# Routed attention and a gated feed-forward block: when and how the weights are converted, and how the first batch is laid out

## The chip, the cores and the metric

The kernel runs on one core of one Trainium2 chip. The core has TensorE for matrix products (PE; PEld is its weight load), VectorE (DVE), ScalarE (ACT) and GpSimd (POOL) for elementwise work, and SyncE (SP), whose queue issues transfers. Each engine takes its instructions in the order of its own queue; engines wait for one another through semaphores. The metric is the device time of one execution in microseconds (us); lower is better.

## The reference

Four batches of eight heads, 768 positions of 64 numbers. Each query and key is assigned to the nearest of 16 centroids of its head (cosine similarity), and a query attends only to keys of its own cluster. The result goes through a feed-forward block (ffn) of width 2048. The weights w_in (512 x 2048) and w_out (2048 x 512) arrive as 64-bit floating point, the rest as 32-bit.

```python
q_assign = np.argmax(np.einsum('bhsd,hcd->bhsc', q_n, c_n), axis=-1)
k_assign = np.argmax(np.einsum('bhsd,hcd->bhsc', k_n, c_n), axis=-1)
mask = q_assign[:, :, :, None] == k_assign[:, :, None, :]
scores = np.where(mask, scale * np.matmul(q, k.transpose(0, 1, 3, 2)), -1e9)
attn = softmax(scores)                  # with 1e-9 in the denominator
x = np.matmul(attn, v)                  # (B,H,S,D) -> (B*S, H*D)
h = x @ w_in
g = h * erf(softplus(h))
out = (g @ w_out).astype(np.float32)
```

## The kernel before

**Pairs, units, chunks.** Two heads are handled together as a pair; 16 pairs (four to a batch), each of 12 units: a half of the queries (384 columns, HW) by one block j of 128 keys, six blocks to a half. The feed-forward block works in 12 chunks of 256 rows, three to a batch.

**Per pair.** `route` (L239) transposes q and k on VectorE (L244), copies a bf16 version of both into the mask operands `qm` and `km` on GpSimd (L246), clears one row of `qm` (L250), multiplies by the centroids (psim, L255), and finds the nearest one with operations on VectorE and one product with `rank` on GpSimd (L262 to L286); the one-hot result goes into `qm` on VectorE (L292) and into `km` on ScalarE (L294). `shift` (L299) makes twelve bf16 products (sm, L306), takes the maximum of each row on VectorE (L310), turns the twelve columns into a row (nm L315, pn L320, nmT L322), and writes this row into `qm` by way of a DRAM tile (two issues, L324 and L327). Together they are `aside(p)`, a generator whose every `yield` is one step: four of `route`, twelve maxima and a last step.

**Per unit.** `scores` (L340): two f32 products and two bf16 mask products into one PSUM tile, Exp on ScalarE (L358) into one of eight `pr` tiles, and a running sum `acc` on GpSimd (L362, L366). The tiles of sc and sm share two PSUM buffers (pool `ps_s`). `attend` (L370) runs once per half: the products with v (av, L377), the row sums (psum, L384), a division made from Ln, Exp and VectorE operations (L390 to L395), and the result xT (L406).

**Feed-forward.** `hidden(n)` (L434) makes h in eight groups (hp, L442, copied out by VectorE, L449) and ends in `gate(n)`: Softplus and Erf on ScalarE (L425), the product on VectorE (L427). `project(n)` (L456) multiplies by w_out (po, L461), copies (L468) and writes out (L469). `ffn_stream` yields the cost of each matmul; chunk n starts only when all four pairs of its batch are done, and the products of `project(n - 1)` are woven into `hidden(n)`.

**Weights.** `convert` (L157) handles 1024 columns of f32 result: a 1 MB load issued from GpSimd's queue (L159) into one of two buffers, Square on ScalarE (L165), and seven VectorE operations (L166 to L185) that put the bits of the 64-bit number together to a 32-bit one. There are 16 such steps, eight for w_in and eight for w_out.

**Order.** `aside(0)` comes first. Then a loop over the units in twos: `attend` of the half before, at j = 2; `scores` twice; in the first four pairs one `convert`, except at j = 2; then five slots (SLOTS), each of which pumps ffn matmuls worth `per_slot` cycles and takes one step of the next pair's `aside`. This is the order in which the program is traced. A scheduler then orders the instructions of each engine by its own estimate of when they are ready, unless an instruction is marked to keep the order of the program; only the load of an activation table (L234) is so marked. The pools of the ffn (`g`, `a_s`, `osb`) are opened at the end of the first batch, where the conversion's buffers are closed (L528, L529), in the same memory.

Of the kernel before, what the change touches and what calls it, by code (L numbers as in the profile page):

```python
# [17 lines left out]
P = 128  # L18
# [14 lines left out]
LC = 1024  # L33
TINY_HI = 2.0**-15 * 1.125
# [6 lines left out]
SLOTS = 5  # L41


@with_exitstack
def kernel(
# [11 lines left out]

    def pool(name, bufs, **kw):
        return ctx.enter_context(tc.tile_pool(name=name, bufs=bufs, **kw))
# [8 lines left out]
    xTp = pool("xTp", 1)  # L68
    linep = pool("linep", 2, space=bass.MemoryType.DRAM)
# [51 lines left out]
    wpool = ExitStack()  # L121
    setup = wpool.enter_context(tc.tile_pool(name="setup", bufs=1))
    cen = setup.tile([P, D], F32, name="cen")
# [4 lines left out]
    nc.vector.tensor_copy(out=identb, in_=ident)  # L128
    nc.vector.memset(minus, -1.0)

    for c in range(C):
        nc.vector.memset(rank[0:D, c : c + 1], float(C - c))
        nc.vector.memset(rank[D:P, c : c + 1], BIG * (C - c))
    nc.vector.memset(ccT, 0.0)
    nc.vector.memset(alleps, S * EPS)

    for e in range(2):
        nc.vector.reduce_sum(
            out=own[:, e : e + 1],
            in_=ident.rearrange("p (g x c) -> p x g c", x=2, c=C)[:, e], axis=AX.XY,  # L140
        )
    for t in lows:
        nc.gpsimd.memset(t["q"], 0.0)
        nc.gpsimd.memset(t["k"], 0.0)
        for e in range(2):
            nc.gpsimd.memset(t["k"][e * D + SH : e * D + SH + 1, e], 1.0)
    for t in prs:
        nc.gpsimd.memset(t[:, :, HW : HW + 2], EPS)
# [5 lines left out]
    wraw = wpool.enter_context(tc.tile_pool(name="wraw", bufs=2))  # L154
    wtmp = wpool.enter_context(tc.tile_pool(name="wtmp", bufs=2))

    def convert(dst, src):  # L157
        raw = wraw.tile([P, LC, 2], U32, name="raw64")
        nc.gpsimd.dma_start(out=raw.rearrange("p (a n) w -> p a (n w)", a=src.shape[1]), in_=src)  # L159
        hi, lo = raw[:, :, 1], raw[:, :, 0]  # L160
        m = wtmp.tile([P, LC], U32, name="w_m")
        x = wtmp.tile([P, LC], U32, name="w_x")
        mf, xf = m.bitcast(F32), x.bitcast(F32)

        nc.scalar.activation(out=xf, in_=raw.bitcast(F32)[:, :, 1], func=ACT.Square)  # L165
        nc.vector.tensor_scalar(  # L166
            out=x.bitcast(I32), in0=xf, scalar1=TINY_HI**2, scalar2=-1.0,
            op0=ALU.is_ge, op1=ALU.mult,
        )

        nc.vector.tensor_scalar(
            out=m, in0=hi, scalar1=3, scalar2=0x7FFFFFFF,
            op0=ALU.logical_shift_left, op1=ALU.bitwise_and,
        )
        nc.vector.scalar_tensor_tensor(  # L175
            out=m, in0=m, scalar=0x40000000, in1=x, op0=ALU.bitwise_xor, op1=ALU.bitwise_and
        )
        nc.vector.tensor_scalar(
            out=x, in0=m, scalar1=0x7F800000, scalar2=None, op0=ALU.bitwise_and
        )  # L180
        nc.vector.scalar_tensor_tensor(
            out=xf, in0=lo, scalar=2.0**-52, in1=xf, op0=ALU.mult, op1=ALU.mult
        )
        nc.vector.tensor_tensor(out=xf, in0=mf, in1=xf, op=ALU.add)
        nc.vector.scalar_tensor_tensor(  # L185
            out=dst.bitcast(U32), in0=hi, scalar=0x80000000, in1=x,
            op0=ALU.bitwise_and, op1=ALU.bitwise_or,
        )

    w_steps = []  # L190
    for c in range(0, DFF, LC):
        for r in range(DM // P):
            rows = moe_w_in[r * P : (r + 1) * P, 2 * c : 2 * (c + LC)]
            w_steps.append((w_in[:, r, c : c + LC], rows.unsqueeze(1)))
    n = LC // DM
# [372 lines left out]
```

The softmax here doesn't subtract the row's maximum and nothing guards it: scores larger than these inputs give would overflow.

## Time and profile before

| | |
|---|---|
| time, median of 6 runs | 1354.16 us (1352.52 to 1356.17) |
| the profiled execution | 1356.17 us, of which 1354.4 us are the span from the first to the last instruction |
| mean granted TensorE clock | 0.943 |
| PE busy | 1190.4 us (88%) |
| DVE busy | 656.9 us (49%) |
| ACT busy | 476.5 us (35%) |
| POOL busy | 414.4 us (31%) |
| chain that ended last | PE 67%, DVE 16%, ACT 8% |
| conversion of weights on DVE | 152 us (sum of the groups of L166 to L185) |
| ffn products on PE (hp, po) | 758 us |

The profile is one execution. Busy times are summed over the span and so over stages with different limits; a matmul's record overlaps its neighbour's, so a busy PE is not PE at its peak. The granted clock is the share of its full speed at which TensorE ran.

### The profile page before, as it was taken

What the parts mean: (1) busy time and instruction counts of PE and PEld (TensorE: products, weight loads), DVE (VectorE), ACT (ScalarE), POOL (GpSimd) and SP (SyncE); (2) the same over time, 40 slices, a digit from 0 to 9 for tenths busy, and PEclk for the clock granted to TensorE, in tenths of its full rate; (3) what the DMA queues carried; (4) which work ended last, traced back from release to release, by engine and by line L of the source; (5) the groups of instructions that cost most, each with busy time, mean ns of one, the idle gap of its engine ahead of it and who ended that gap; (6) DMA issues with size and microseconds to landing.
All of it is one profiled execution on the core that took longest, in us unless ns stands there. A gap on an engine that the chain in (4) does not pass through costs nothing.

```text
span 1354.4 us, 12507 instructions
## 1 busy us (share of the span) xinstructions
PE 1190.4 (88%) x4881; PEld 629.6 (46%) x4881; DVE 656.9 (49%) x924; ACT 476.5 (35%) x516; POOL 414.4 (31%) x310
## 2 busy tenths in 40 slices
PE   1676676679999899879999989889999999999998
PEld 0122222236546445344554635544644646575764
DVE  5989999974443525441634443442625302221221
ACT  2223222234335425432543633423534524330321
POOL 5335546351424233423233231424242221100000
PEclk9878777879899999989999989989999999999999
DMA  5312243220101011201011010101000000000000
GB/s 121 97 58 71 71 119 86 74 36 1 24 20 32 12 27 25 36 0 32 20 18 26 18 26 16 35 1 32 21 0 28 1 8 8 8 8 8 8 16 15
DMA packets 132875, 42.88 MB, mean 32 GB/s; under 512 B 126640, under 2 KB 126672, under 8 KB 131792
## 3 DMA queue, kind: packets, MB, share of 16 engines
q1 hardware_dynamic: 129488, 25.31, 9.2%
q0 software_dynamic: 3328, 16.78, 3.6%
q8 instruction: 38, 0.62, 0.2%
q14 instruction: 21, 0.17, 0.0%
HBM read 35.73 MB, written 6.34 MB: 31 GB/s over the span
## 4 chain that ended last, share of the span: by engine, by line
PE 67%; DVE 16%; ACT 8%; issue 4%; POOL 3%; DMA 1%; POOLq 0%; DVEq 0%; ACTq 0%
PE po L461 24%; PE hp L442 21%; PE sc L347 8%; PE av L377 7%; PE sm L306 4%; DVE nmx L310 2%; PE sc L353 1%; ACT pr L358 1%; DVE g L427 1%; ACT L390 1%; PE psum L384 1%; ACT km L294 1%; DVE hot L281 1%; POOL acc L366 1%; DVE w_m L175 1%
## 5 line engine op out<-in xcount | busy, mean ns | idle before, releaser
L442 PE MATMUL hp<-xT,w_in 128*128 128x256 f32 x1536 | 383.9, 387 | 2.8 <-DVE g L449 2.8
L461 PE MATMUL po<-w_out,g 128*128 128x512 f32 x768 | 374.3, 607 | 10.4 <-DVE g L449 7.7
L366 POOL TENSOR_TENSOR acc<-acc,pr 128x768 f32<-128x768 f32 x128 | 229.7, 1794 | 451.2 <-ACT pr L358 446.2
L442 PEld LDWEIGHTS hp<-xT,w_in 128*128 128x128 f32 x1536 | 290.3, 193 | 118.7 <-issue 80.7
L358 ACT ACTIVATE pr<-sc 128x768 f32<-128x768 f32 x192 | 151.6, 808 | 323.9 <-PE sc L353 323.2
L310 DVE TENSOR_REDUCE nmx<-sm 128x2 f32<-128x768 f32 x192 | 180.2, 953 | 108.4 <-PE sm L306 107.0
L347 PE MATMUL sc<-qT,kT 64*128 64x384 f32 x768 | 192.6, 558 | 25.2 <-DVE nmx L310 19.0
L461 PEld LDWEIGHTS po<-w_out,g 128*128 128x128 f32 x768 | 142.1, 192 | 130.7 <-issue 104.9
L449 DVE COPY g<-hp 128x512 f32<-128x512 f32 x96 | 65.9, 686 | 237.8 <-PE hp L442 237.8
L377 PE MATMUL av<-pr,in_v 128*64 128x386 f32 x768 | 159.5, 523 | 22.4 <-DVE xT L406 11.4
L306 PE MATMUL sm<-km,qm 128*128 128x384 bf16 x384 | 104.8, 359 | 84.6 <-ACT pr L358 33.7
L347 PEld LDWEIGHTS sc<-qT,kT 64*128 64x128 f32 x768 | 70.5, 201 | 106.9 <-DVE nmx L310 44.1
L306 PEld LDWEIGHTS <-qm 128*128 128x128 bf16 x384 | 36.7, 102 | 166.4 <-issue 152.6
L362 POOL TENSOR_TENSOR acc<-pr,pr 128x768 f32<-128x768 f32 x32 | 61.6, 1926 | 162.3 <-ACT pr L358 161.9
L377 PEld LDWEIGHTS av<-pr,in_v 128*64 128x64 f32 x768 | 56.0, 143 | 109.5 <-issue 94.0
L425 ACT ACT_TABLE_LOAD x48 | 61.6, 1283 | 103.0 <-DVE g L449 102.2
L392 DVE SCALAR_TENSOR_TENSOR den<-psum,inv 128x384 f32<-128x384 f32 x32 | 17.8, 557 | 150.7 <-ACT inv L391 150.7
L427 DVE TENSOR_TENSOR g<-a_s,g 128x512 f32<-128x512 f32 x96 | 67.6, 757 | 23.4 <-ACT a_s L425 23.4
L425 ACT ACTIVATE a_s<-g 128x2048 f32<-128x2048 f32 x24 | 45.9, 1910 | 69.9 <-DVE g L449 69.8
L353 PE MATMUL sc<-qm,km 64*128 64x384 bf16 x384 | 69.9, 342 | 0.0
L294 ACT COPY km<-hotT 32x384 bf16<-32x384 bf16 x64 | 32.5, 508 | 90.3 <-DVE hotT L286 89.6
L425 ACT ACTIVATE a_s<-a_s 128x2048 f32<-128x2048 f32 x24 | 45.8, 1910 | 0.3
(74 smaller groups left out, 723.4 us busy)
## 6 DMA issues: line engine op xcount, KB each, us to landing
raw<-in_moe_w_in_dram POOLq DMA_DIRECT2D x8, 1024.0 KB, 5.7
raw<-in_moe_w_out_dram POOLq DMA_DIRECT2D x8, 1024.0 KB, 5.3
in_q<-in_q_dram SPq DMA_DIRECT2D x64, 96.0 KB
in_k<-in_k_dram SPq DMA_DIRECT2D x64, 96.0 KB
in_v<-in_v_dram SPq DMA_DIRECT2D x32, 192.0 KB
out_dram<-osb SPq DMA_DIRECT2D x24, 256.0 KB
qm<-line SPq DMA_DIRECT2D x32, 1.5 KB
line<-nmT SPq DMA_DIRECT2D x16, 3.0 KB
```

The lines of the kernel that those rows point to most:

```text
L306: nc.tensor.matmul(sm[:, e, 0:HW], lhsT=st["qm"][:, e, t * P : (t + 1) * P], rhs=st["km"][:, e, half * HW : (half + 1) * HW], start=True, ...
L310: nc.vector.tensor_reduce(out=nmx[:, t, half], in_=sm[:, :, 0:HW], axis=AX.X, op=ALU.max, negate=True)
L347: nc.tensor.matmul(sc[:, e, 0:HW], lhsT=st["kT"][r, j * P : (j + 1) * P], rhs=st["qT"][r, cols], start=True, stop=False,)
L353: nc.tensor.matmul(sc[:, e, 0:HW], lhsT=st["km"][r, e, j * P : (j + 1) * P], rhs=st["qm"][r, e, cols], start=False, stop=True,)
L358: nc.scalar.activation(out=pr[:, :, 0:HW], in_=sc[:, :, 0:HW], func=ACT.Exp, scale=D**-0.5)
L366: nc.gpsimd.tensor_tensor(out=st["acc", half], in0=st["acc", half], in1=pr[:, :, 0:HW], op=ALU.add)
L377: nc.tensor.matmul(av[e * D : (e + 1) * D], lhsT=st["v"][:, j, e], rhs=prs[(u0 + j) % NPT][:, e], start=(j == 0), stop=(j == NJ - 1),)
L425: nc.scalar.activation(out=s[:, i : i + half], in_=src[:, i : i + half], func=func)
L427: nc.vector.tensor_tensor(out=h[:, i : i + GW], in0=s[:, i : i + GW], in1=h[:, i : i + GW], op=ALU.mult)
L442: nc.tensor.matmul(hp[:, a], lhsT=w_in[:, r, f0 : f0 + P], rhs=xTs[b * HP + r][c], start=(r == 0), stop=(r == HP - 1),)
L449: nc.vector.tensor_copy(out=gs[n][:, fp * GW : (fp + 1) * GW], in_=hp)
L461: nc.tensor.matmul(po, lhsT=gs[n][:, ft, tt * P : (tt + 1) * P], rhs=w_out[:, ft], start=(ft == 0), stop=(ft == NFT - 1),)
```

## The change

- **Conversion.** A step is 512 columns (LC), 16 steps for w_in and 16 for w_out. In place of Square and seven VectorE operations, a step has Abs on ScalarE, a maximum and an integer addition on GpSimd (`clamp`), and five VectorE operations. The 64-bit data is loaded from SP's queue (`fetch`), for w_in into quarters of the two `g` tiles, for w_out into the half tiles `a_s` of the gates; the results m and x lie in the same places. `convert` is a generator that yields after each VectorE operation; `prepare(n)` takes n of these steps.
- **When.** The 16 steps of w_in are spread over the first aside and the first four pairs, 36 operations before the first scores and then 11 a pair. Those of w_out follow in the second batch, two operations after each pump. `hidden` and `project` are traced no further than the weights are converted.
- **First batch.** The loop over units goes one slot at a time, 12 slots of preparation and 48 with scores; `aside` of the next pair, `prepare` and `attend` (two units behind the scores) have fixed places. `te`, `ve`, `ae` and `ge` mark every instruction they issue to keep the program's order, up to slot 44 (FIRST). Two PSUM tiles alternate for av, one of them from the ffn's pool. In the last four slots the ffn is pumped, 16 matmuls of chunk 0 each.
- **Routing.** The copies into `qm` and `km` and the clearing of the row move from GpSimd to ScalarE. The transposes of q and k are one step. v is loaded before the maxima instead of after. In the later batches the steps of `aside` have chosen slots (ASIDE) out of 30.
- **Mask products.** `scores` takes one or two units; for two it makes the f32 products of both first, then the mask products of both.
- **Feed-forward.** A chunk starts when the halves that it reads are done. `project(0)` is not woven into `hidden(1)` but follows it. The gate has two half tiles instead of one whole; there is one output tile instead of two. `attend` is one unit, and `divide` is split off it, in two steps.

```diff
-LC = 1024
-TINY_HI = 2.0**-15 * 1.125
+LC = 512
+TINY_HI = 2.0**-15
+ASIDE = (0, 2, 4, 6, *range(9, 9 + 2 * NJ), 10 + 2 * NJ)
+FIRST = 2 * NJ * HP - 4
+class InOrder:
+    def __getattr__(self, name):
+        def call(*args, **kw):
+            ins = getattr(self.engine, name)(*args, **kw)
+            if self.on[0]:
+                self.tc.keep_in_program_order(ins)
+            return ins
+        return call
...
-    def convert(dst, src):
-        raw = wraw.tile([P, LC, 2], U32, name="raw64")
-        nc.gpsimd.dma_start(out=raw.rearrange("p (a n) w -> p a (n w)", a=src.shape[1]), in_=src)
...
+    room = [gp.tile([P, NFT, TB], F32, name="g") for _ in range(2)]
+    def fetch(n):
+        if n in steps or n >= len(w_steps):
+            return
+        if n < n_w_in:
+            t = room[n // 2 % 2][:, n % 2 * (NFT // 2) : (n % 2 + 1) * (NFT // 2)]
+        else:
+            t = half_tile()
+        t = t.rearrange("p f t -> p (f t)").bitcast(U32)
+        nc.sync.dma_start(out=t[:, 0 : 2 * LC], in_=w_steps[n][1])
+        raw = t[:, 0 : 2 * LC].rearrange("p (n w) -> p n w", w=2)
+        steps[n] = raw[:, :, 1], raw[:, :, 0], t[:, 2 * LC : 3 * LC], t[:, 3 * LC : 4 * LC]
+    def clamp(n):
+        if n < len(w_steps):
+            hi, _, _, x = steps[n]
+            ae.activation(out=x.bitcast(F32), in_=hi.bitcast(F32), func=ACT.Abs)
+            ge.tensor_scalar(
+                out=x.bitcast(F32), in0=x.bitcast(F32), scalar1=TINY_HI, scalar2=None, op0=ALU.max
+            )
+            ge.tensor_tensor(
+                out=x.bitcast(I32), in0=x.bitcast(I32), in1=bias.to_broadcast([P, LC]), op=ALU.add
+            )
+    def convert():
+        clamp(0)
+        clamp(1)
+        for n in range(len(w_steps)):
+            hi, lo, m, x = steps[n]
+            mf, xf = m.bitcast(F32), x.bitcast(F32)
+            ve.tensor_scalar(out=m, in0=x, scalar1=3, scalar2=None, op0=ALU.logical_shift_left)
+            yield
+            if n + 3 < n_w_in:
+                fetch(n + 3)
+            elif n < n_w_in:
+                fetch(n_w_in)
+                fetch(n_w_in + 1)
+            else:
+                fetch(n + 1)
+            ve.tensor_scalar(out=x, in0=m, scalar1=0x7F800000, scalar2=None, op0=ALU.bitwise_and)
+            yield
+            if n + 2 <= n_w_in + 1:
+                clamp(n + 2)
+            ve.scalar_tensor_tensor(
+                out=xf, in0=lo, scalar=2.0**-52, in1=xf, op0=ALU.mult, op1=ALU.mult
+            )
+            yield
+            ve.tensor_tensor(out=xf, in0=mf, in1=xf, op=ALU.add)
+            yield
+            ve.scalar_tensor_tensor(
+                out=w_steps[n][0].bitcast(U32), in0=hi, scalar=0x80000000, in1=x,
+                op0=ALU.bitwise_and, op1=ALU.bitwise_or,
+            )
+            if n > n_w_in:
+                clamp(n + 1)
+            converted[0] = n + 1
+            yield
...
     def route(p):
...
-            for e in range(2):
-                nc.gpsimd.tensor_copy(out=low[nm][(1 - e) * D : (2 - e) * D, e], in_=raw[e * D : (e + 1) * D])
...
+        for nm in "qk":
+            for e in range(2):
+                ae.copy(
+                    out=low[nm][(1 - e) * D : (2 - e) * D, e], in_=st[nm + "T"][e * D : (e + 1) * D]
+                )
+        yield
...
+        for e in range(2):
+            row = low["q"][e * D + SH : e * D + SH + 1, e]
+            ae.mul(out=row, in_=row, mul=0.0)
         yield
...
     def hidden(n):
...
         for fp in range(NFT // GW):
+            while converted[0] < DM // P * ((fp + 1) * GW * P // LC):
+                yield None
...
     def ffn_stream():
...
-            while (n // CPB + 1) * HP > len(xTs):
+            b, c = n // CPB, n % CPB
+            halves = range(c * TB // HW, ((c + 1) * TB - 1) // HW + 1)
+            while not all((b * HP + r, h) in done for r in range(HP) for h in halves):
                 yield None
...
-                if i >= 2 * GW * HP:
+                i += cost is not None
+                if n > 1 and i > 2 * GW * HP:
...
+    for slot in range(-2 * NJ, 2 * NJ * HP):
+        in_order[0] = slot < FIRST
+        p, r = divmod(slot + 2 * NJ, 2 * NJ)
+        if slot >= 0:
+            scores([slot])
+        if r == 0:
+            ready[p] = aside(p)
+        prepare(3 if slot < 0 else (1, 3, 1)[r] if r < 3 else 3 if r > 9 else 0)
+        for _ in range(1 if r < 4 or r == 10 else 2 if r < 10 else 0):
+            next(ready[p])
+        if slot >= 2:
+            if (slot - 2) % NJ == 0 and slot > 2:
+                next(part)
+            attend(slot - 2, other=(slot - 2) // NJ % 2 == 1 and slot < FIRST - 2)
+            if (slot - 2) % NJ == NJ - 1:
+                part = divide(slot - 2)
+                next(part)
+        if slot >= FIRST:
+            pump(4 * NFT * TB)
...
+    for u in range(2 * NJ * HP, len(units), 2):
         p, half, j = units[u]
...
+        scores([u, u + 1])
+        for i in range(SLOTS):
             pump(per_slot)
-            next(ahead, None)
-    attend(nu - NJ)
+            prepare(2)
+            if (half * NJ + j) // 2 * SLOTS + i in ASIDE:
+                next(ahead, None)
```

## The prediction

> **What bounds the kernel now.** I read the 40 slices first. Each digit is the busy tenths of 34 us.
>
> ```profile
> PE   1676676679999899879999989889999999999998
> ...
> DVE  5989999974443525441634443442625302221221
> ```
>
> VectorE (DVE) is full in slices 3 to 8 while TensorE (PE) is at 6 to 7 tenths; from the tenth slice on it is the reverse. So there are two kernels in one span. Busy time by stretch (microseconds and instructions of each engine, then the granted clock) puts numbers on it; I cut where the first scores (44.6) and the first copy out of hp (305) stand in the timeline:
>
> ```profile
> core 0: us, PE busy (x) PEld busy (x) DVE busy (x) ACT busy (x) POOL busy (x), PEclk, DMA share, GB/s
> 0.00:44.60 44.60, 12.15 (x35) 3.54 (x35) 30.74 (x85) 8.22 (x10) 20.72 (x36) 1.00 0.50 122
> 44.60:305.00 260.40, 180.43 (x702) 63.19 (x703) 234.76 (x257) 74.11 (x106) 127.49 (x87) 0.80 0.28 75
> 305.00:1160.00 855.00, 807.58 (x3525) 445.33 (x3525) 352.20 (x524) 351.21 (x374) 266.17 (x188) 0.97 0.09 19
> ```
>
> The second row is the first batch, four pairs in 260.4 us, 65 us a pair: DVE is busy 90%, PE 69% at a clock of 0.80. The third row is PE bound: 94% busy. What DVE does in the second row is the conversion of the weights; the groups by shape give it (count, busy, mean ns):
>
> ```profile
> L175 DVE SCALAR_TENSOR_TENSOR w_m<-w_m,w_x 128x1024 uint32<-128x1024 uint32 x16 | 25.2, 1575 | 0.1
> L184 DVE TENSOR_TENSOR w_x<-w_m,w_x 128x1024 f32<-128x1024 f32 x16 | 24.8, 1549 | 0.1
> ...
> L181 DVE SCALAR_TENSOR_TENSOR w_x<-raw,w_x 128x1024 f32<-128x1024 uint32 x16 | 23.5, 1467 | 0.2
> ...
> L178 DVE TENSOR_SCALAR w_x<-w_m 128x1024 uint32<-128x1024 uint32 x16 | 18.0, 1124 | 0.1
> ...
> L171 DVE TENSOR_SCALAR w_m<-raw 128x1024 uint32<-128x1024 uint32 x16 | 17.1, 1073 | 9.2 <-DMA raw<-in_moe_w_in_dram 9.2
> L166 DVE TENSOR_SCALAR w_x<-w_x 128x1024 int32<-128x1024 f32 x16 | 16.9, 1056 | 0.5 <-ACT w_x L165 0.5
> ```
>
> One step of 1024 columns is 1.06+1.07+1.58+1.12+1.47+1.55+1.65 (L185, mean of its two forms) = 9.5 us; some fifteen of the sixteen steps fall in the second row, 142 of its 235 us. What is left, 93 us, is 23 us a pair: routing 7.2 us (two transposes 1.91, sims 0.58, mx 0.55, compare 0.69, mr 0.55, hot 1.14, hotT 0.58, qm 1.23), twelve maxima at 0.95 = 11.4 plus nm 0.4, two divisions at 2.2.
>
> **The change, part by part.** *VectorE.* A step becomes five operations on 512 columns. L171 and L178 stand for the shift and the mask, L181, L184, L185 stay; halved means give 0.54+0.56+0.73+0.77+0.83 = 3.4 us. But the means hold waits that need not halve. The same operation takes 0.56 or 2.03 (start, us, instruction):
>
> ```profile
> 161.22 2.03 DVE L395 SCALAR_TENSOR_TENSOR den<-den,inv 128x384 f32<-128x384 f32 x1
> ...
> 301.40 0.56 DVE L395 SCALAR_TENSOR_TENSOR den<-den,inv 128x384 f32<-128x384 f32 x1
> ```
>
> A POOL addition (L366, 160.69 for 2.14 us) lies beside the first, none that long beside the second (L366 starts at 301.55). Quiet durations of the conversions in the timeline are 0.66 (L171, L178) and 1.2; half of these plus the full excess of each mean gives 0.33+0.41+0.33+0.46+0.6+0.27+0.6+0.35+0.6+0.45 = 4.4 us. I take 4, between ends 3.4 and 4.4. The Trainium skill, SBUF — State Buffer, section "SBUF: two separate sides", has the pair of ports that VectorE and GpSimd share as an exclusive lock held for a whole instruction; it speaks against giving GpSimd two more operations a step, and by it the 4.4 would be the value and the sum 3 us longer (0.4 for each of the 7.2 steps ahead of the first scores).
>
> In twelve slots of a pair 11 operations are pinned, 2.2 steps: 8.8 us instead of 36. DVE then has 23+9 = 32 us a pair and stops being the bound.
>
> *PE, a pair at full clock*, from rows near 546 to 572 us: scores 0.91 to 1.12 a unit (11 to 13), attention values 4.11 for 24 matmuls (8.2 for 48), twelve maxima tiles at 0.49 (5.9), psum 1.6, psim 0.9, pn 0.2: 28 to 30.
>
> *ACT* takes four casts from POOL (L246; nearest rows 0.51 for 384 columns, 0.81 for 768: bounds 0.5 to 1.0, I take 0.8 as the width is 768), two clearings of a row of 768 (0.25 to 0.81, I take 0.8) and Abs of 512 strided columns (half of 1.15 to 1.15, 0.6). *POOL* loses casts and memsets (5 us a pair) and gets max (0.5 to 1.1, taken 0.8; casts at 0.99) and an integer addition (L272 1.12 at 384, L366 1.79 at 768: 1.1 to 1.8, taken 1.3): 2.1 us a step, 4.6 a pair. Neither is a bound: ACT some 21 us a pair, POOL 24.
>
> *The pinned order, so the chain of a pair.* With r counting slots, 0 at the start of a pair:
> - r 0 to 3. Scores 1.1, next scores to 2.9, Exp of r=1 ends at 3.85. ACT now has four casts behind it (3.2), then Ln and Exp of the division (1.1): 8.15. Only then Exp of r=2 (8.9), on which POOL's addition of r=2 waits (1.8), and behind that in POOL's queue the rank product (1.1): 11.8. Then DVE mr, hot, hotT (2.3) and ACT km (2.0): 16.3. The first maxima matmul at r=4 waits for it; PE ran dry at about 10.2. The matmul goes at 16.5, 1.1 after its slot's scores could have: 15.4 us from r=0 to r=4, with 6.3 us of PE idle. All later scores and values are queued behind that matmul.
> - r 4 to 9. Two score buffers serve a score and two maxima: 1.12 + Exp with its signals 1.06 + 0.49 + 0.69 = 3.3 a slot, 19.8; plus 0.5 where DVE's division (2.2) delays the maxima of r=9.
> - r 10 and 11. Three conversions (2.1 at least) stand before nm on DVE, so PE's transpose waits some 2.2 us; the row's two DMAs took from 48.0 to before 50.6 in the trace, 2.6 us, and land as the next pair's mask products want them: 6.0 us for both slots.
> The fetches moved to SP's queue wait for nothing here (step n+3 takes the place of n-1, done), and v's issue, now ahead of the maxima, finds its buffer free since r=1; 512 KB ahead of the row's DMAs would cost up to 2.7 us a pair (half of 5.3).
>
> Sum 41.7. The 6.3 us of idle cost more: after such a gap matmuls run long,
>
> ```profile
> 572.44 0.70 PE L442 MATMUL hp<-xT,w_in 128*128 128x256 f32 x2
> 583.15 0.80 PE L306 MATMUL sm<-km,qm 128*128 128x384 bf16 x2 [10.01 <-ACT pr L358]
> 583.75 2.76 PE L442 MATMUL hp<-xT,w_in 128*128 128x256 f32 x6
> ...
> 590.51 0.49 PE L306 MATMUL sm<-km,qm 128*128 128x384 bf16 x2
> ```
>
> 0.80 or 0.84 for what takes 0.49, for 7 us (583.2 to 590.5) after 10 us idle: about 3 us lost. I add 1.8 for the shorter gap: 43.5 a pair, 174 for four (bounds 38 and 50 a pair). The Trainium skill, TensorE: Matmul & The Clock Gate, Part 1, "What's actually happening", gives half clock after one idle window of about 3.4 us and full clock after one busy window; by that alone 1.7 us a gap, the sum the same within 1 us.
>
> *Start.* Three fetches of 512 KB join SP's queue behind eight q and k issues that end at 5.6. 1 MB took 5.3 to 7.3 us to land, so raw arrives near 11.4; Abs, max and addition (2.7) let DVE begin at 14.3, where it did its transposes at 8.6. From there 36 conversion operations at 0.7 to 0.88 (25 to 32), routing 7.2, maxima 11.8, some 1.5 of waits for POOL, less the last slot's operations that the row's DMAs cover (2.1): the pair's row lands at 58 to 65. With POOL idle of additions there I take the lower part, 59, against 44.6 to the first scores before.
>
> *After slot 48.* Before, this is 1354.4-305 = 1049.4 us. Two units of scores, values and one psum had been done by 305 and are still to do: +4. The four last slots are not pinned and hold hidden(0); its work is the same but fills their waits (0.6+0.6+2.2): -3.5. Converting w_out, 16 x 4 = 64 us of DVE, is planned two operations a pump, two steps per 12.5 us (a pair is 75 us there), so 100 us long; DVE was 41% busy in that row (352/855) and comes to 100%. Copies out of hp and maxima will queue: +10 (0 if PE's other work hides it; 35 if half of the 64 shows). An earlier start of each chunk shortens the gap at the batch boundary (10.01 us idle above, and its slow clock): -10 (0 to -20). Products in twos: two units back to back took 1.81, apart 2.24, but PE mostly had them back to back already: -1 (0 to -14). ACT's added 5 us a pair lie under PE's 75 us; without that cover they would cost 60. One output tile instead of two costs nothing while a po takes 14.5 us (32 at 0.45); without that it is 24 times the 3.4 us of the last output (1351.0 to 1354.4). Sum 1049.
>
> 59+174+1049 = 1282 us of span. The profiled run took 1356.17 for its span of 1354.4, 1.8 more, and lies 2.0 above the median of the six; the two cancel: 1282.
>
> **Rivals.** (1) *The chain at r=0 to 3 is hidden and PE alone bounds the first batch*, 34 us a pair: 59+136+1049 = 1244. For it: every engine's sum is below 33 us. Against: ACT's queue order, which is fixed. 12%.
> (2) *The first batch stays half slow*: the clock stays at 0.80, 29/0.8 = 36 us of PE work a pair, and with the same waits (12.7) and conversions at 4.4 about 52: 59+208+1049 = 1316. For it: every gap over 4 us in the trace is followed by slow matmuls. Also what comes if the pins don't tighten the order. 13%.
> (3) *w_out comes too late; slower than before.* Its raw blocks and the gates share two half tiles, and fetches are on SP's queue, ahead of the row of shifts, q, k, v and the outputs. If the gates (two ACT passes and products, 14 us each) leave one tile, a step is serial: landing 2.8 to 5.7, Abs 0.6 to 1.15, POOL 1.6 to 2.9, DVE 3.4 to 4.4: 8.4 to 14.1 against the planned 6.25. Each excess is paid 16 times by PE, which holds project(0) in order: at 12 us 16x5.75 = 92, so 1374. It decides from 6.25+72/16 = 10.8 us a step. Against: two tiles overlap steps, and hidden(1) gives 28 us of other work. 6%.
>
> **How the numbers follow.** The forecast has 69%. The six runs lie within 0.2% of their median, about what a measurement of this kernel can tell from no change; that bounds same. Range 1245 to 1330: pairs at 38 give 1260, at 50 1308, the other ends (-24, +35) added partly; it takes in (2) and the upper edge of (1), and leaves out (3), half of (1) and the tails, under 2 in 10. The forecast's own range is 1260 to 1310. Faster holds all but (3): 0.93; same 0.01; slower 0.06.
>
> **What would show it.** First score matmuls at 56 to 65 us; four pairs at 43 us, DVE near 75% in them; the longest PE idle of each pair before the first maxima matmul, waiting for km or qm; w_out's conversions between 235 and 350 us with DVE at nine tenths; the last 190 us as before. Wrong if pairs take over 55 us, or PE waits for w_out by tens of us.

## The result and the profile after

The changed kernel takes 1356.91 us (median of 21 runs, 1355.01 to 1359.61), the kernel before 1353.81 us in the same sessions: a ratio of 1.0024, 95% interval 1.0018 to 1.003. It is 0.2% slower; the forecast was 1282.

The page of the changed kernel, the 40 slices (34 us each):

```profile
PE   1376766987878999799999899999999999999998
...
DVE  7956768449686345634443535435344513221221
...
POOL 6445545226353222421222222222222222100000
```

VectorE is no longer full in slices 3 to 8, as forecast. But TensorE is hardly busier there up to slice 7, and in slices 10 to 13, where it had stood at 9, it is at 7 and 8. Its windows (columns as in the prediction), cut at the first scores and at the conversion of w_out:

```profile
0.00:60.50 60.50, 12.79 (x36) 3.53 (x36) 49.62 (x100) 16.32 (x23) 37.83 (x43) 1.00 0.57 144
60.50:255.00 194.50, 135.49 (x623) 44.55 (x623) 134.90 (x184) 77.13 (x111) 91.13 (x57) 0.87 0.20 39
...
300.00:440.00 140.00, 111.67 (x415) 55.43 (x415) 107.86 (x144) 53.58 (x64) 65.85 (x45) 0.86 0.20 58
440.00:1160.00 720.00, 682.83 (x2991) 371.86 (x2988) 311.50 (x447) 334.10 (x371) 189.35 (x111) 0.99 0.10 19
```

In the second row no engine is the bound: TensorE 70%, VectorE 69%, so a chain of waits sets the time. The third row shown repeats that on a smaller scale while w_out is converted (TensorE 80%, clock 0.86). From 440 us on it is TensorE alone.

The first of the two issues of the maxima row (`line<-nmT`), one per pair, marks how far a kernel is. From the timelines of SyncE's queue (start, us):

| kernel | row 1 | 2 | 3 | 4 | 5 | 6 | 7 | 16 |
|---|---|---|---|---|---|---|---|---|
| before | 48.0 | 95.1 | 154.3 | 217.5 | 277.6 | 328.5 | 405.5 | 1056.9 |
| after | 60.9 | 107.3 | 155.2 | 204.3 | 272.6 | 372.0 | 450.2 | 1093.9 |
| scale_pins | 49.1 | 95.6 | 143.1 | 189.0 | 253.9 | 348.2 | 414.9 | 1056.8 |
| five_scale | 44.0 | 92.9 | 140.5 | 178.9 | 232.4 | 326.3 | 390.3 | 1036.3 |

After row 4 the changed kernel does hidden(0), which the kernel before does later; so the rows alone mislead, and I count TensorE's records by tile. At 300 us it had 146 matmul records into hp where before had 14, and 302 scores records against 312. The 132 records at 0.216 us less ten scores at about 0.2 make it some 26 us ahead. At 460 us it had 296 against 292 of hp, 72 against 64 of po, but 432 against 456 of scores and 264 against 288 of av: level, or a few us behind. **The head start was earned and then lost between 300 and 460 us.** Both run level from there.

### The profile page after: what moved, and what is told of

Its sections match the earlier page's. It is cut to its first block, busy times and chain, and to the rows that moved or that the text cites. A ratio compares the mean times of both kernels' runs of the same rounds, so it can differ in the third digit from the quotient of the medians.

```text
span 1357.1 us, 12573 instructions
## 1 busy us (share of the span) xinstructions
PE 1177.5 (87%) x4881; PEld 621.2 (46%) x4881; DVE 658.1 (48%) x958; ACT 553.5 (41%) x626; POOL 395.8 (29%) x262
## 4 chain that ended last, share of the span: by engine, by line
PE 54%; DVE 19%; ACT 13%; issue 8%; POOL 4%; DMA 1%; SPq 0%; ACTq 0%; DVEq 0%; POOLq 0%
PE po L56 21%; PE hp L56 16%; PE sc L56 7%; PE av L56 5%; DVE g L56 5%; DVE nmx L56 4%; ACT L56 3%; PE sm L56 3%; ACT a_s L56 3%; ACT pr L56 2%; DVE a_s L56 2%; ACT inv L56 2%; ACT km L56 2%; DVE den L56 2%; ACT qm L56 2%
## 5 line engine op out<-in xcount | busy, mean ns | idle before, releaser
L56 PE MATMUL po<-w_out,g 128*128 128x512 f32 x768 | 376.0, 610 | 15.0 <-DVE w_out L56 12.5
L56 POOL TENSOR_TENSOR acc<-acc,pr 128x768 f32<-128x768 f32 x128 | 224.2, 1752 | 478.7 <-ACT pr L56 463.2
L56 ACT ACTIVATE pr<-sc 128x768 f32<-128x768 f32 x192 | 147.9, 807 | 326.2 <-PE sc L56 325.8
L56 PE MATMUL sc<-qT,kT 64*128 64x384 f32 x768 | 180.7, 556 | 18.3 <-DVE nmx L56 11.9
L56 PE MATMUL av<-pr,in_v 128*64 128x386 f32 x768 | 151.4, 511 | 0.0
L56 PEld LDWEIGHTS av<-pr,in_v 128*64 128x64 f32 x768 | 50.2, 139 | 76.4 <-issue 76.0
L56 PE MATMUL sc<-qm,km 64*128 64x384 bf16 x384 | 59.7, 337 | 6.7 <-DMA qm<-line 6.7
L56 ACT ACTIVATE a_s<-a_s 128x2048 f32<-128x2048 f32 (+1 forms) x40 | 56.6, 1415 | 21.5 <-DMA a_s<-in_moe_w_out_dram 21.2
```

The source lines that it names most:

```text
L56: ins = getattr(self.engine, name)(*args, **kw)
```

## The experiments

Each edit is against the changed kernel unless said otherwise. All were compared with the kernel before on the same chip (1352.6 to 1354.3 us).

| label | us | ratio to before, 95% interval |
|---|---|---|
| no_w_out | 1324.33 | 0.9784 [0.9769, 0.9799] |
| w_out_one_op | 1352.22 | 0.9989 [0.9979, 1.0] |
| w_out_dve_only | 1339.43 | 0.9906 [0.9883, 0.9928] |
| w_out_clamp_only | 1349.32 | 0.9964 [0.995, 0.9977] |
| gate_first | 1357.53 | 1.0034 [1.0021, 1.0047] |
| five_ops_in_before | 1376.8 | 1.017 [1.0154, 1.0185] |
| seven_ops_late | 1337.87 | 0.9888 [0.9868, 0.9909] |
| no_pins | 1341.29 | 0.9917 [0.99, 0.9933] |
| seven_late_no_pins | 1323.45 | 0.9781 [0.9765, 0.9797] |
| seven_all_no_pins | 1311.64 | 0.9694 [0.9679, 0.9708] |
| seven_all_pins | 1336.85 | 0.9876 [0.9861, 0.9891] |
| spread | 1352.51 | 0.9983 [0.9962, 1.0004] |
| one_by_one | 1368.37 | 1.0108 [1.0084, 1.0131] |
| seven_dummy_pool | 1355.24 | 1.0009 [0.9999, 1.0019] |
| five_scale | 1303.81 | 0.9624 [0.9611, 0.9637] |
| five_paced_pool | 1321.99 | 0.9772 [0.9759, 0.9785] |
| scale_pins | 1323.13 | 0.9773 [0.9759, 0.9786] |

**What the conversion of w_out costs where it now stands.** no_w_out fills w_out with a constant:

```diff
-        for n in range(len(w_steps)):
+        for n in range(n_w_in):
...
+        for n in range(n_w_in, len(w_steps)):
+            for i in range(4):
+                yield
+            ge.memset(w_steps[n][0], 0.01)
```

> The changed kernel with the conversion of w_out left out: no loads of it, no Abs, no maximum, addition and no VectorE operations; a GpSimd memset writes a constant into each of the 16 blocks instead, so the output isn't the reference's. Theory A, the head start of the first batch is given back while w_out is converted in the second batch: at 300 us the changed kernel stood about 29 us ahead by its matmul counts, at 460 us 6 us behind, so 1357-35 = 1322 us, down to 1310 if the slower clock goes too. Rival B, it is lost to the new order of the later batches (spread asides, products in twos, chunk 0 ahead): 1345 us or more.

33 us less than the changed kernel: as theory A had it. That is the whole price of w_out's conversion where it stands. Next, of the five VectorE operations of a w_out step only the last is kept (w_out_one_op); only the five are kept, on data that is already there, without loads, Abs and GpSimd (w_out_dve_only); or the loads, Abs and GpSimd are kept and a copy on GpSimd takes the place of the five (w_out_clamp_only).

```diff
-            ve.tensor_scalar(
+            full = n < n_w_in
+            full and ve.tensor_scalar(
...
+            else:
+                m, x = spare_m, w_steps[n][0].bitcast(U32)
+                hi = lo = w_in[:, 0, 0:LC].bitcast(U32)
...
+            else:
+                ge.tensor_copy(out=w_steps[n][0], in_=xf)
```

> The changed kernel with loads, Abs, maximum and addition for w_out kept, but only the last of its five VectorE operations; the output isn't the reference's. If the price is VectorE's time (four operations of 0.4 to 0.7 us, 16 times, some 36 us with waits): within 8 us of the run without any conversion of w_out. If the price is the chain of load, Abs and two GpSimd operations through the two half tiles that the gates share: within 10 us of 1357.

> The changed kernel with w_out's loads, Abs, maximum and addition left out and all five VectorE operations a step kept, fed from weights that are there already; the output isn't the reference's. The run with one VectorE operation left was only 5 us faster than the changed kernel, the run without the conversion 33 us. If the price is the queues of ScalarE and VectorE standing at an instruction that waits for a load or for GpSimd: 1324 to 1334 us. If it is VectorE's load after all: 1345 us or more.

> The changed kernel with w_out's loads, Abs, maximum and addition kept, and a GpSimd copy of the result in place of the five VectorE operations, so that VectorE never waits for the clamp; the output isn't the reference's. If VectorE's standing before w_out's operations is the larger part: 1328 to 1338 us. If ScalarE's standing at Abs for the load, with the Exps behind it, and GpSimd's additions behind the clamp are: 1342 to 1355 us.

Four of five VectorE operations gone: 5 us of the 33. Everything but the five gone: 17 us, between the two forecasts. VectorE's part gone altogether: 8 us, so 25 of the 33 remain without VectorE, though GpSimd's copies (10.6 us in all) have come in. The parts don't add up, but most of the price is not VectorE's time alone: it comes with what stands in front of it. The fourth kernel asks whether that is the half tile shared with the first gate; it fetches and clamps the first two blocks only after that gate.

```diff
-            elif n < n_w_in:
-                fetch(n_w_in)
-                fetch(n_w_in + 1)
-            else:
+            elif n >= n_w_in:
...
     in_order[0] = False
+    for n in (n_w_in, n_w_in + 1):
+        fetch(n)
+        clamp(n)
```

> The changed kernel with the first two loads of w_out and their clamps traced after the gate of chunk 0 instead of before it, so that this gate doesn't wait for w_out's half tiles; the loads come some 10 to 15 us later. If the shared half tiles at the first gate are a large part of the 33 us: 1335 to 1350 us. If not: 1355 to 1370 us, by the later start.

No change: the tile shared with the first gate is not it. The later gates share it too, and were not tried.

**The form of the conversion.** five_ops_in_before puts Abs, maximum, integer addition and the five operations into the kernel before, at 1024 columns, and nothing else.

```diff
-        nc.scalar.activation(out=xf, in_=raw.bitcast(F32)[:, :, 1], func=ACT.Square)
...
+        nc.scalar.activation(out=xf, in_=raw.bitcast(F32)[:, :, 1], func=ACT.Abs)
+        nc.gpsimd.tensor_scalar(out=xf, in0=xf, scalar1=TINY_HI, scalar2=None, op0=ALU.max)
+        nc.gpsimd.tensor_tensor(
+            out=x.bitcast(I32), in0=x.bitcast(I32), in1=bias.to_broadcast([P, LC]), op=ALU.add
```

> The kernel before with the new form of conversion alone (Abs on ScalarE, maximum and addition on GpSimd, five VectorE operations, still 1024 columns, 16 steps in the first batch). Theory: the first batch is bound by VectorE, which loses 16 x (9.5 - 6.5) = 48 us of its 235; most of it shows: 1305 to 1325 us. Rival: the first batch is bound by chains through several engines, and GpSimd's 4 us a step more come in its place: 1345 us or more.

It is 23 us slower where the theory expected a gain; its rival (1345 us or more) held. Its window over the first batch and two groups (count, busy us, mean ns, then idle before):

```profile
44.60:305.00 260.40, 158.68 (x635) 54.98 (x633) 211.80 (x211) 70.61 (x99) 177.65 (x107) 0.76 0.27 74
```

```profile
L169 POOL TENSOR_SCALAR w_x<-w_x 128x1024 f32<-128x1024 f32 x16 | 46.2, 2886 | 31.0 <-ACT w_x L168 30.9
...
L174 DVE TENSOR_SCALAR w_m<-w_x 128x1024 uint32<-128x1024 uint32 x16 | 23.9, 1499 | 23.4 <-POOL w_x L170 23.4
```

VectorE is relieved by 23 us (211.8 for 234.8) and TensorE does 22 us less in the same time. GpSimd has 50 us more (177.7 for 127.5), VectorE waited 23.4 us for its results, and the shift takes 1.50 us where the old form's took 1.07. So the old form goes into the changed kernel: for w_out (seven_ops_late), for both weights (with no pins, below).

```diff
+            if n >= n_w_in:
+                ae.activation(out=x.bitcast(F32), in_=hi.bitcast(F32), func=ACT.Square)
+                return
...
+                ve.tensor_scalar(
+                    out=x.bitcast(I32), in0=xf, scalar1=(TINY_HI * 1.125) ** 2, scalar2=-1.0,
+                    op0=ALU.is_ge, op1=ALU.mult,
+                )
```

> The changed kernel with w_out's 16 steps in the old form (Square on ScalarE, seven VectorE operations, nothing on GpSimd); w_in as changed. GpSimd's 2.5 to 3.2 us a step go out of the chain, 1 to 1.5 us of VectorE come in, in a batch where VectorE has room. If the chain's length is the price: 1335 to 1350 us. If the loads and the shared half tiles are: 1350 to 1365 us.

19 us less than the changed kernel.

**The pins.** no_pins leaves every order to the scheduler.

```diff
-    in_order = [True]
+    in_order = [False]
...
-        in_order[0] = slot < FIRST
+        in_order[0] = False
```

> The changed kernel with no instruction marked to keep the program's order; all else as changed. My prediction put four pairs of the first batch at 43.5 us with the pins. If the pins are what makes the first batch shorter (48 us a pair measured, 65 before): over 1370 us. If the lighter conversion and the slots as traced do it: within 10 us of 1357.

16 us less. Neither forecast held: the order by hand is worse than the scheduler's. The two edits together, and the old form for w_in as well:

> The changed kernel without pins and with w_out's steps in the old form (seven VectorE operations, Square, nothing on GpSimd). Alone the first gave 16 us and the second 19. If they are two losses at two places (first batch and second): 1319 to 1328 us, the fastest so far. If both are the same slack in the schedule: 1333 to 1342 us.

> As the run without pins and with w_out in the old form, but w_in's steps in the old form too, so nothing of the conversion is on GpSimd anywhere. VectorE gets 16 x 1.3 = 21 us more before and in the first batch, GpSimd loses 16 x 2.6 = 42 us. If the lighter VectorE work shortens the first batch: 8 to 20 us slower than the run with w_out alone in the old form. If GpSimd's two operations cost what they save: within 5 us of it.

> The old form of conversion everywhere, with the pinned order of the change up to slot 44; nothing is left out. Theory A: the pins cost 12 to 18 us whatever the conversion, since the chain at the start of a pair waits for its ScalarE casts and its nearest-centroid row in a fixed order: 1324 to 1330, the first four pairs at 45 us or more each. Rival: the pins cost only because the longer steps of the five-operation form stand in the fixed order ahead of routing and maxima; in the old form they cost nothing: within 4 us of 1311.6.

seven_late_no_pins came as the sum of its edits. seven_all_no_pins was expected to lose 8 to 20 us, or to stay within 5, and gained 12 more. seven_all_pins puts the pins back, for 25 us, outside the 12 to 18 of its theory: under pins the form of w_in makes 1 us of difference (1337.87 to 1336.85), without them 12. The two costs overlap.

spread does two things at once: no conversion stands directly before nm (three did, at r = 10), and a pair takes 20 operations instead of 11, so that seven of w_out's sixteen steps are done in the first batch:

```diff
-        prepare(3 if slot < 0 else (1, 3, 1)[r] if r < 3 else 3 if r > 9 else 0)
+        prepare(3 if slot < 0 else (1, 3, 1, 0, 2, 2, 2, 2, 2, 2, 0, 3)[r])
```

> The changed kernel with more conversion operations pinned in the first batch: two in each of the slots r = 4 to 9, none at r = 10 (ahead of nm), 20 a pair instead of 11, so seven of the sixteen w_out steps are done before the second batch. If VectorE idles 1.3 us in each of these slots (two maxima are 1.97 of 3.25 us) and the loss is that of converting w_out later: 7/16 of 35 us and up to 2 us a pair before nm, so 1333 to 1345 us. If the first batch has no room: 1357 us or more.

4 us less than the changed kernel, between its two forecasts; against the kernel before, its interval reaches 1. Clearing the place before nm and converting part of w_out earlier are worth little together; what each does by itself was not tried.

**Products in twos.** `scores([u, u + 1])` is taken apart into two calls.

> The changed kernel with the score products of the later batches traced one unit after the other as before, not in twos. I put the twos at -1 us (0 to -14). If they help: 1358 to 1371 us. If they cost: under 1353.

11 us more, as forecast if they help: the twos are worth 11.

**By which way the five-operation form costs.** Is it GpSimd's time, or the longer chain from load to product? seven_dummy_pool adds to seven_all_no_pins two operations a step on a tile that nobody waits for.

```diff
+                ge.tensor_scalar(out=dummy, in0=dummy, scalar1=TINY_HI, scalar2=None, op0=ALU.max)
+                ge.tensor_tensor(
+                    out=dummy.bitcast(I32), in0=dummy.bitcast(I32), in1=bias.to_broadcast([P, LC]), op=ALU.add
+                )
```

> The kernel with the old form of conversion everywhere and nothing pinned (1311.6), plus two GpSimd operations a step, a maximum and an integer addition over 512 columns, on a tile of its own that nothing waits for; nothing is left out. Theory A: the five-operation form costs by what it adds to GpSimd, whose queue also holds the running sums and the products with rank, and by VectorE running longer beside it: 32 steps of 2.8 us put back most of the 29 us between 1311.6 and no_pins (1341.3): 1328 to 1345, with the shift or mask near 0.7 instead of 0.46 us. Rival: the price is the longer chain from load through ScalarE, GpSimd and VectorE to the product that waits; operations that nobody waits for then cost under 6 us: 1310 to 1318.

It costs 44 us, more than its theory allows (1328 to 1345), and doesn't decide: on its page the slices of GpSimd begin

```profile
POOL 9994434313042222322212222222222222100000
```

The scheduler put what waits for nothing at the very front, and row 1 came at 76.9 us instead of 50.0. The pair that follows avoids this. five_scale takes no_pins and drops both GpSimd operations, by a factor in ScalarE's Abs; five_paced_pool adds their time again, reading weights of steps that are already finished.

```diff
-            ae.activation(out=x.bitcast(F32), in_=hi.bitcast(F32), func=ACT.Abs)
-            ge.tensor_scalar(
-                out=x.bitcast(F32), in0=x.bitcast(F32), scalar1=TINY_HI, scalar2=None, op0=ALU.max
-            )
-            ge.tensor_tensor(
-                out=x.bitcast(I32), in0=x.bitcast(I32), in1=bias.to_broadcast([P, LC]), op=ALU.add
-            )
+            ae.activation(out=x.bitcast(F32), in_=hi.bitcast(F32), func=ACT.Abs, scale=2.0**-112)
...
+            k = n - 3 if n <= n_w_in + 1 else n - 1
+            past = dummy if k < 0 else w_steps[k][0]
+            ge.tensor_scalar(out=dummy, in0=past, scalar1=TINY_HI, scalar2=None, op0=ALU.max)
```

> no_pins (1341.3) without the two GpSimd operations of a step: a factor of 2^-112 in ScalarE's Abs takes the place of the integer addition, and the maximum is left out, so numbers below 2^-120 come out as zero. Five VectorE operations, one ScalarE operation and no GpSimd operation are left of a step. Theory A: the two GpSimd operations are the whole price of the five-operation form: at or below the old form's 1311.6, 1302 to 1314. Rival: the form costs by something else, such as the loads or Abs: 1325 or more.

> five_scale plus the maximum and the integer addition, on a tile of their own that nothing waits for; the maximum reads the weights of a step that was finished before, so that it can't run earlier than in no_pins. Theory A (GpSimd's time and VectorE slower beside it): at least two thirds of the difference between five_scale and no_pins come back: 1328 to 1345. Rival (the longer chain of dependent operations): under one third comes back: below 1320.

> The changed kernel (1357) with pins, without the two GpSimd operations of a step, as in five_scale. Theory A: 1328 to 1338, what seven_all_pins takes (1336.9) less a few us of VectorE's time; the first four pairs stay at 45 us or more, since their chain doesn't hold these operations. Rival: in the pinned order the GpSimd operations are what makes a pair long: below 1322, pairs of 42 us or less.

five_scale is the fastest of all, 1303.81 us, 3.8% under the kernel before, inside theory A; it changes only numbers under 2^-120. Against no_pins that is 37.5 us for 64 GpSimd operations. Their time without the dependence brings 18 of these back: between the two thirds of theory A and the third of its rival. So about half of the price is GpSimd's time with VectorE slowed beside it. The other half, 19 us, is put down to the longer chain by difference only. scale_pins shows the operations at 34 us in the changed kernel itself, and the pins at 19 us (1323.13 against 1303.81). At 1323 it lies between theory A (1328) and its rival (1322), but its first four pairs took 48 us each, so the operations are not what makes a pair long.

## Why the prediction was wrong

The profiled span is 1357.1 us, 75 over the forecast of 1282. First scores began at 60.5 us; the fifth pair's at 287.7, of which 27.6 are hidden(0)'s 128 matmuls at 0.216; so 60.5 + 199.6 + 1097.0 against 59 + 174 + 1049: **+1.5, +25.6 and +48.**

**What held.** First scores at 60.5 us, inside 56 to 65. VectorE at 69% in the first batch, near the forecast 75. A step's VectorE time, 4.1 us for w_in against 4. And the chain of a pair; TensorE's timeline in the second pair (start, us, instruction, idle before it and what ended that):

```profile
128.32 1.01 PE L56 MATMUL sm<-km,qm 128*128 128x384 bf16 x2 [5.66 <-ACT km L56]
...
154.65 0.27 PE L56 MATMUL pn<-identb,nm 128*12 128x128 bf16 x1 [3.38 <-DVE nm L56]
...
161.29 0.50 PE L56 MATMUL sc<-qm,km 64*128 64x384 bf16 x2 [1.45 <-DMA qm<-line]
```

The wait for km before the first maxima is 5.66 us (6.3 forecast), that for nm 3.38 (2.2). ScalarE's queue before it is as read from the code: casts, Ln and Exp of the division, then Exp of r=2, and at last km:

```profile
116.32 1.67 ACT L56 CAST qm<-qT 64x768 bf16<-64x768 f32 x2
118.00 1.67 ACT L56 CAST km<-kT 64x768 bf16<-64x768 f32 x2
119.70 0.58 ACT L56 ACTIVATE inv<-psum,alleps 128x384 f32<-128x384 f32 x1
...
120.74 0.79 ACT L56 ACTIVATE pr<-sc 128x768 f32<-128x768 f32 x1
...
127.76 1.57 ACT L56 COPY km<-hotT 32x384 bf16<-32x384 bf16 x3 [3.67 <-DVE hotT L56]
```

**First batch, +25.6.** The chain of a pair was right, two of its terms were not. (a) "The row's two DMAs took from 48.0 to before 50.6 in the trace, 2.6 us": now the mask product comes 5.1, 5.8 and 6.1 us after the row's first issue, 9 us more over three pairs. SyncE's queue at the third row, then VectorE's, show what stands between:

```profile
155.24 0.34 SPq L402 DMA_DIRECT2D line<-nmT  x1
159.05 0.34 SPq L139 DMA_DIRECT2D in_q<-in_q_dram  x1
159.49 0.65 SPq L405 DMA_DIRECT2D qm<-line  x2
```

```profile
155.69 0.69 DVE L56 SCALAR_TENSOR_TENSOR g<-g 128x512 f32<-128x512 uint32 x1
156.42 1.50 DVE L56 TENSOR_TENSOR g<-g 128x512 f32<-128x512 f32 x1
158.04 0.98 DVE L56 STREAM_TRANSPOSE qT<-in_q 128x768 f32<-128x768 f32 x1
```

The second issue comes 4.25 us after the first, behind a load of q; before, it came 1.3 to 1.6 us after (2.75 once). The load fills the buffer that the transpose of q reads. It goes out as the transpose ends (159.02), and the transpose stands in VectorE's queue behind conversions. In the second row it is the same (4.0 us). In the first (2.3 us) a fetch of w_in stands between and goes out at 62.63, as a conversion on VectorE ends (62.61). SyncE's waits from 100 to 170 us name the same releasers: the loads of q waited 6.5 us for the transpose, the fetches 71.8 us for conversions, which costs only where the row's second issue stands behind. So "The fetches moved to SP's queue wait for nothing here" was wrong, and the load of q was given no wait. The 2.7 us allowed for loads ahead of the row had the right size by luck: it stood for data on the way, not for a wait in the queue. No run takes this wait away by itself. (b) The fourth pair took 55.8 us (204.3 to the end of the batch without hidden(0)), 12 over the forecast. VectorE's and TensorE's timelines there:

```profile
210.75 3.02 DVE L56 TENSOR_SCALAR g<-g 128x512 uint32<-128x512 uint32 x2
...
214.71 0.68 DVE L56 TENSOR_SCALAR g<-g 128x512 uint32<-128x512 uint32 x1
215.31 1.52 DVE L56 TENSOR_TENSOR g<-g 128x512 f32<-128x512 f32 x1
...
219.13 0.69 DVE L56 SCALAR_TENSOR_TENSOR w_in<-g 128x512 uint32<-128x512 uint32 x1
219.74 0.58 DVE L56 STREAM_TRANSPOSE sims<-psim 128x384 f32<-128x384 f32 x1
```

```profile
220.46 1.55 PE L56 MATMUL psum<-acc,minus 128*64 128x384 f32 x4 [7.95 <-DVE sims L56]
```

The last steps of w_in stand one behind another, and the routing of the fifth pair behind them; TensorE waits 7.95 us, the longest wait of that pair. Between the transposes and sims the program has four of these operations; ten ran. The other six belong to the last two slots of the pair, which aren't pinned, and the scheduler put them ahead. "In twelve slots of a pair 11 operations are pinned" didn't ask where operations go that are not pinned. The first step of w_out went ahead in the same way, to before the first scores: its shift, at 58.41, had waited 2.50 us for GpSimd, with nm of the first pair behind it in VectorE's queue.

The pins themselves were counted as a gain: rival (2) asked what comes if they "don't tighten the order", no term asked whether they lengthen the waits. Without pins the kernel ends 14 to 25 us sooner (four pairs of kernels), and TensorE's waits show where. scale_pins, then five_scale, 60 to 460 us (sum, times, longest):

```profile
PE sm L56 <- ACT km L56: 18.9, 5, 6.0
...
PE pn L56 <- DVE nm L56: 8.6, 5, 3.4
...
PE sc L56 <- DVE nmx L56: 6.7, 8, 2.8
...
PE psum L56 <- DVE sims L56: 5.2, 1, 5.2
PE sc L56 <- ACT pr L56: 3.7, 1, 3.7
```

```profile
PE sc L56 <- DVE nmx L56: 16.6, 15, 6.0
PE sm L56 <- ACT pr L56: 12.4, 5, 3.5
PE sc L56 <- ACT pr L56: 11.9, 5, 3.7
...
PE psum L56 <- DVE sims L56: 1.4, 1, 1.4
```

The waits for km and nm, 27.5 us, all but vanish in the unpinned kernel (nm 0.3). In their place it has more waits for maxima (16.6 for 6.7) and of scores for Exp (11.9 for 3.7). All waits together are 74 us with pins and 55 without.

**GpSimd's two operations.** "max (0.5 to 1.1, taken 0.8; casts at 0.99)", and 1.3 for the addition; the groups of the changed kernel say

```profile
L56 POOL TENSOR_SCALAR g<-g 128x512 f32<-128x512 f32 x16 | 27.1, 1695 | 21.0 <-ACT g L56 21.0
L56 POOL TENSOR_SCALAR a_s<-a_s 128x512 f32<-128x512 f32 x16 | 25.0, 1561 | 27.6 <-ACT a_s L56 27.6
...
L56 POOL TENSOR_TENSOR g<-g,bias 128x512 int32<-128x512 int32 x16 | 17.2, 1076 | 1.3
```

2.8 us a step instead of 2.1, outside the upper end taken for the maximum. And the old form was known only from its crowded place: 9.5 us per 1024, so 4.75 per 512. In the new place (seven_all_no_pins, to 300 us) it takes 0.52+0.46+0.68+0.46+0.69+0.78+0.83 = 4.4 us, the new form 4.1. So the five operations save 0.3 us of VectorE and cost 2.8 us of GpSimd. The "8.8 us instead of 36" a pair came mostly from fewer steps, 2.2 a pair where the old 36 us are 7.5 of 512 columns: w_out was moved to the second batch, and 7.2 steps of w_in stand before the first scores.

**The step that failed** is "Neither is a bound: ACT some 21 us a pair, POOL 24". It took GpSimd's operations as load on an engine with room. After the first scores it gave them no term: not for VectorE standing before a step that GpSimd hasn't finished, nor for what stands behind that step. scale_pins, whose profiled run is 37 us shorter than the changed kernel's (the medians 34), puts their price at 12 us before the first scores (48.7 for 60.5), 7 in the first batch (192.7 for 199.6) and 18 later. The 12 were in the forecast; the 25 were not.

The forecast had the first 12 us in "Abs, max and addition (2.7)" ahead of VectorE's start and in "36 conversion operations at 0.7 to 0.88". The working for 0.88 compared two rows of L395; an addition of 1.95 us lay beside the short one too, beginning 0.15 us after it, so the two rows differ not by the addition's length but by which began first (160.69 for 161.22 in the long one). The direction was right: without GpSimd's operations a step of w_in takes VectorE 3.4 us (scale_pins), with them 4.1. The first step's shift and mask with and without GpSimd beside them, changed kernel, then scale_pins:

```profile
14.22 1.70 DVE L56 TENSOR_SCALAR g<-g 128x512 uint32<-128x512 uint32 x2 [4.79 <-POOL g L56]
```

```profile
10.96 0.89 DVE L56 TENSOR_SCALAR g<-g 128x512 uint32<-128x512 uint32 x2 [1.51 <-ACT g L56]
```

**After slot 48, +48.** "Copies out of hp and maxima will queue: +10 (0 if PE's other work hides it; 35 if half of the 64 shows)": this term was mis-sized, the price is 33 (no_w_out), at the upper end. The 18 us that go with GpSimd's operations in this stretch (above) overlap with it. A step that isn't ready stops VectorE's queue with all that stands behind it (VectorE's, then TensorE's waits of the changed kernel, 300 to 460 us):

```profile
DVE a_s L56 <- POOL a_s L56: 11.2, 6, 3.3
```

```profile
PE po L56 <- DVE w_out L56: 12.5, 3, 5.1
PE sc L56 <- DVE nmx L56: 7.5, 6, 2.8
```

This is rival (3), "w_out comes too late", in a milder form. The conversions, forecast between 235 and 350 us with VectorE at nine tenths, ran until 429 us with VectorE at 77% (300 to 440). The last fourteen steps came 8.9 us apart: more than the planned 6.25, less than the 10.8 from which that rival takes over, and products waited 12.5 us for w_out, not 92. Of the 48 us 23 follow from this term (33 for 10). Products in twos were taken at 1 us (0 to 14) and are worth 11, so 35 us stay open. The -10 for the batch boundary is not simply missing: from 460 us on, maxima products waited 23.9 us for Exp before (longest 10.0), 4.6 after. But other waits, for copies out of hp, maxima and nm, took their place, and all waits of TensorE there are 40 us before and 36 after. The casts moved to ScalarE, the chosen slots of `aside`, the half tiles of the gate and the single output tile were not tried by themselves. five_scale, without GpSimd's operations and without pins, still takes 22 us more than 1282.

**Rival (2)**, 52 us a pair, was nearest for the first batch (49.9), but not by its mechanism: the clock was 0.87, not 0.80, and the time went into the waits above.

## What to carry to other kernels

When work is taken from a busy engine and given to another, price the operation as it runs in its new place, compare it with the old form in that same place, and ask what stands in the receiving queue behind it. Where a step passes through three engines before a product, a step that isn't ready stops a queue that also holds other work. And an order by hand has to beat the scheduler's in a run of its own before it is built on: here the same work ended 14 to 25 us sooner without it.

## What the runs showed of the hardware

- A maximum with a constant over 128x512 f32 took GpSimd 1.56 to 1.70 us, longer than the addition of two integer operands (1.08 to 1.10, the second a column broadcast); at 1024 columns 2.89 (five_ops_in_before). The Trainium skill, GPSIMD Engine Reference, section "3.1 Elementwise — side-by-side cycle accounting", has about 2.6 cycles an element for two operands, which its other figures turn into an estimate of 1.1 us at 512: that is what the addition took. Section "4.1 Engine selection" sends an elementwise maximum to VectorE and calls one-operand work on GpSimd roughly line rate. No run here has the maximum on VectorE; the second is not borne out, since one operand and a constant took longer than two operands.
- A shift or mask on VectorE over 512 columns took 0.46 us (mean, to 300 us) in seven_all_no_pins and 0.75 in seven_dummy_pool, which adds GpSimd's two operations; in the changed kernel 0.76, in scale_pins, without them, 0.53. The Trainium skill's exclusive lock, cited in the prediction for 3 us, fits the sign; no run here tells it from another reason for the slower operations.
